# Attention memory with two MoE layers on one core: token order of the last block's gates, its stores on two queues, its last products by tile

## The chip, the cores and the metric

The kernel runs on one core of a Trainium2 chip. The metric is the device time of one execution in microseconds; the median of three runs stands for a kernel. A profile of one more execution gives the span from the first to the last instruction of the core, with every instruction and DMA in it.

## What is computed

Three parts follow on each other. An attention with a memory of 32 slots (4 batches, 8 heads, 576 positions, 64 features a head) gives x of 2304 tokens by 512 features. A gated layer (`_moe_ref`) normalizes x and takes it through 1536 gates back to 512. The last layer, which the change touches, is this:

```python
def _moe2_ref(x, w_in, w_out):          # x: (2304, 512), w_in: (512, 2048), w_out: (2048, 512)
    h = x @ w_in
    beta = 1.0
    neg = h <= -beta
    pos = h >= beta
    g = np.where(pos, h, np.where(neg, 0.0, (h + beta) ** 2 / (4.0 * beta)))
    return (g @ w_out).astype(np.float32)
```

Inputs and output are float32. The kernel splits each operand of a product into a high part, rounded to the matmul's type, and the rest (gh and gl, wh and wl, xh and xl), and takes three products for one: high by high, high by low, low by high.

## The kernel before

The first part and the gated layer are laid out by a planner with costs and due times (`Agenda`). The change touches neither. Their result x lies in DRAM as two matrices, high and low, of 512 features by 2304 tokens. The tokens stand there in an order of their own: first, for each batch, its 512 first positions (in the order j, p, where the position is 4p + j), then the last 64 positions of all four batches (in the order batch, j, p, where the position is 512 + 2p + j, with j of 2 and p of 32).

The last layer runs over five blocks of tokens: blocks 0 to 3 are the 512 first positions of a batch each, block 4 holds the 4 times 64 rest tokens, 256 in all. In a block it runs over 16 chunks of 128 gates (fc).

`p2_in(i, fc)` makes the gates of chunk fc for block i: twelve matmuls (L1032) into a PSUM tile hp, of 512 or 256 columns; then ScalarE's relu into y (L1037), two VectorE steps on y (L1038, L1039), ScalarE's rounding of y into gh (L1042) and VectorE's y minus gh into gl (L1043). In all of them the tokens stand in x's order, so a step is one run of columns.

`p2_out(i, fc)` multiplies a chunk's gates by w_out: for each tile t of 128 tokens (four, in block 4 two) three matmuls (L1057), gh by wh, gh by wl and gl by wh, of 512 columns each, are summed in the PSUM tile acc of t. A tile's sum is complete with chunk 15. It is then copied into osb, for even t by ScalarE (L1066), for odd t by VectorE (L1064), and stored from SyncE's queue. In blocks 0 to 3 that is one store of 128 rows of 2 KB (L1069), every fourth row of the output. In block 4 a tile holds two batches, 64 partitions each, with all 32 tokens of j = 0 ahead of those of j = 1; so there are two stores (L1073), and each writes the rows as j, p, features, which on the DRAM side is 2 by 32 by 512.

The loop at L1084 calls `p2_in` of a chunk and then `p2_out` of the chunk two before it (LAG). The last two rounds have no `p2_in` left: `p2_out` of chunks 14 and 15 of block 4. This part isn't laid out by hand. The framework puts each engine's instructions in an order of its own, by the order of the program and by what its timing model takes to be ready. It also adds the waits.

Of the kernel before, what the change touches and what calls it, by code (L numbers as in the profile page):

```python
# [8 lines left out]
F32R = mybir.dt.float32r  # L9
# [5 lines left out]
P = 128  # L15
# [134 lines left out]
def tile_attn_moe(tc, q, k, v, phi, w_gate, w_val, w_out1, rms_g, w_in2, w_out2, out):  # L150
# [10 lines left out]
    nc = tc.nc  # L161
    B, H, S, D = q.shape
# [11 lines left out]
    SM = P * QJ  # L174
    SL = S - SM
    LJ = 2
# [14 lines left out]
    def pool(stack, name, side):  # L191
        return stack.enter_context(tc.tile_pool(name=name, bufs=1, side=side))
# [772 lines left out]
    def load_w2(i, wp, **place):  # L965
        t = wp.tile([P, 2, 512], F32R, name=f"w2_{i}", **place)
        nc.gpsimd.dma_start(out=t.rearrange("p t f -> p (t f)"), in_=w2_d[i])
        wts[i % 2, i // 2] = (t[:, 0, :], t[:, 1, :])
# [27 lines left out]
    p2g = pool(right, "p2g", "right")  # L996
# [4 lines left out]
    def load_x(i):  # L1001
        c, n = blocks[i]
        xs = []
        for nm, src in (("h", x2h_d), ("l", x2l_d)):
            t = (xb if i else xa).tile([P, KC, SM], F32R, tag=f"x{nm}", name=f"x{nm}{i}", bufs=2 if i else 1)
            nc.gpsimd.dma_start(
                out=t[:, :, 0:n], in_=src[:, c : c + n].rearrange("(c p) t -> p c t", p=P)
            )
            xs.append(t)
        x_t[i] = xs  # L1010
# [11 lines left out]
    xb = pool(left, "xb", "left")  # L1022
    g_t = {}

    def p2_in(i, fc):
        c, n = blocks[i]
        xh, xl = x_t[i]
        wh, wl = (t.rearrange("p (c f) -> p c f", c=KC) for t in wts[0, fc])
        hp = psum.tile([P, 512], F32, tag=f"b{4 + (fc * 2 + fc // 2 % 2) % 4}", name=f"hp{i}_{fc}")[:, 0:n]
        for kc in range(KC):  # L1030
            for x, (wt, xt) in enumerate(((wh, xh), (wh, xl), (wl, xh))):
                nc.tensor.matmul(  # L1032
                    out=hp, lhsT=wt[:, kc, :], rhs=xt[:, kc, 0:n],
                    start=(kc == 0 and x == 0), stop=(kc == KC - 1 and x == 2),
                )
        y = p2.tile([P, SM], F32, tag="y2", name=f"y2_{i}_{fc}", bufs=2)[:, 0:n]
        nc.scalar.activation(out=y, in_=hp, func=AF.Relu, scale=0.5, bias=half)  # L1037
        nc.vector.scalar_tensor_tensor(out=y, in0=y, scalar=1.0, in1=y, op0=ALU.min, op1=ALU.mult)  # L1038
        nc.vector.tensor_tensor(out=y, in0=y, in1=hp, op=ALU.max)  # L1039
        gh = p2g.tile([P, SM], F32R, tag="gh", name=f"gh{i}_{fc}", bufs=2)[:, 0:n]  # L1040
        gl = p2g.tile([P, SM], F32R, tag="gl", name=f"gl{i}_{fc}", bufs=2)[:, 0:n]
        nc.scalar.activation(out=gh, in_=y, func=AF.Copy)  # L1042
        nc.vector.tensor_tensor(out=gl, in0=y, in1=gh.bitcast(F32), op=ALU.subtract)  # L1043
        g_t[i, fc] = (gh, gl)

    acc_t = {}

    def p2_out(i, fc):
        c, n = blocks[i]
        gh, gl = g_t.pop((i, fc))  # L1050
        wh, wl = wts[1, fc]
        if fc == 0:
            acc_t[i] = [psum.tile([P, 512], F32, tag=f"b{t}", name=f"acc{i}_{t}") for t in range(n // P)]
        for t, acc in enumerate(acc_t[i]):
            cs = slice(P * t, P * t + P)
            for x, (gt, wt) in enumerate(((gh, wh), (gh, wl), (gl, wh))):
                nc.tensor.matmul(  # L1057
                    out=acc, lhsT=gt[:, cs], rhs=wt,
                    start=(fc == 0 and x == 0), stop=(fc == NF2 - 1 and x == 2),
                )  # L1060
            if fc == NF2 - 1:
                o = p2.tile([P, DM], F32, tag="osb", name=f"osb{i}_{t}", bufs=2)
                if t % 2:
                    nc.vector.tensor_copy(out=o, in_=acc)  # L1064
                else:
                    nc.scalar.activation(out=o, in_=acc, func=AF.Copy)  # L1066
                if i < B:
                    dst = out[S * i : S * i + SM, :].rearrange("(p j) d -> j p d", j=QJ)[t]
                    nc.sync.dma_start(out=dst, in_=o)  # L1069
                else:  # L1070
                    for z in range(2):
                        r0 = S * (2 * t + z) + SM
                        nc.sync.dma_start(  # L1073
                            out=out[r0 : r0 + SL, :].rearrange("(p j) d -> j p d", j=LJ),
                            in_=o[SL * z : SL * z + SL, :],
                        )

    for i in range(EARLY, NF2):
        load_w2(2 * i, w2b)
    load_x(1)  # L1080
    load_x(2)
    LAG = 2
    seq = [(i, fc) for i in range(len(blocks)) for fc in range(NF2)]
    for z in range(len(seq) + LAG):  # L1084
        if z < len(seq):
            p2_in(*seq[z])
        if z >= LAG:
            p2_out(*seq[z - LAG])
            i, fc = seq[z - LAG]
            if fc == NF2 - 1 and 0 < i and i + 2 < len(blocks):  # L1090
                load_x(i + 2)
        if z == EARLY:
            for fc in range(N2U + N2R, NF2):
                load_w2(2 * fc + 1, wv, tag="raw", bufs=BUFS["raw"])
        if z == NF2 - 1:
            for fc in range(EARLY):
                load_w2(2 * fc, w2b)
# [36 lines left out]
```

## Time and profile before

| what | us |
|---|---|
| median of three runs | 884.05 |
| lowest and highest run | 882.97 and 884.27 |
| the profiled execution | 881.78 |
| its span | 880.0 |
| TensorE busy in the span | 828.8 (94%) |
| VectorE, ScalarE, GpSimd busy | 473.4, 350.8, 179.8 |

The engines have short names in the rows: PE is TensorE's matmul, PEld its weight load, DVE is VectorE, ACT ScalarE, POOL GpSimd, SP SyncE; a q behind a name is the engine's instruction queue, where it issues DMAs and waits. L1057 is line 1057 of the kernel before. A matmul's end is modelled and overlaps the start of the next one. Times of a row are microseconds from the span's start unless a column says ns. A DMA share is the mean busy share of the core's sixteen DMA engines.

### The profile page before, as it was taken

The page shows a single profiled execution, that of the slowest core. Times are in us where ns is not written, and L with a number is a line of the kernel's source. Part 1 is how long each engine was busy: PE and PEld are TensorE (multiplying, and loading weights), DVE is VectorE, ACT ScalarE, POOL GpSimd, SP SyncE. Part 2 cuts the span into 40 slices and gives each one's busy share as a digit, 9 for nine tenths or more (in the row PEclk, how much of TensorE's full clock was granted, in tenths as well). Part 3 has the DMA queues.
Part 4 walks back from the last instruction along what each step waited for, and adds up shares of the span by engine and source line. Part 5 has one row for each costly group of instructions (what it writes and reads, how often), then busy time and mean ns, then how long its engine had stood idle before and what let it go on. Part 6 is the DMA issues. An engine that isn't in the chain of part 4 may idle for free.

```text
span 880.0 us, 15147 instructions
## 1 busy us (share of the span) xinstructions
PE 828.8 (94%) x6058; PEld 724.1 (82%) x6058; DVE 473.4 (54%) x817; ACT 350.8 (40%) x695; POOL 179.8 (20%) x207
## 2 busy tenths in 40 slices
PE   7996797799999999999999999999999999999993
PEld 5885576589999999999998888888888888888892
DVE  3679989974875488357413333433343334333441
ACT  1466786752664477356302222222222222222331
POOL 3257855431312222123303200000000000000000
PEclk9999899699999999999999999999999999999997
DMA  9965757747578688776956920100040003000100
GB/s 323 327 203 187 244 192 262 271 140 245 192 252 305 223 277 275 238 250 228 353 195 209 400 93 1 48 1 0 5 140 1 0 5 91 1 0 1 48 1 24
DMA packets 72143, 137.56 MB, mean 156 GB/s; under 512 B 8841, under 2 KB 37513, under 8 KB 72073
## 3 DMA queue, kind: packets, MB, share of 16 engines
q1 hardware_dynamic: 61576, 108.28, 36.4%
q0 software_dynamic: 10496, 28.32, 10.3%
q8 instruction: 47, 0.77, 0.4%
q14 instruction: 24, 0.19, 0.1%
HBM read 99.35 MB, written 37.22 MB: 155 GB/s over the span
## 4 chain that ended last, share of the span: by engine, by line
PE 85%; DVE 6%; DMA 2%; issue 2%; ACT 2%; POOL 1%; SPq 0%; POOLq 0%; DVEq 0%; ACTq 0%
PE acc L1057 23%; PE hp L1032 23%; PE ops L864 17%; PE vps L806 7%; PE gps L806 7%; PE vwps L757 2%; PE xp L678 1%; DMA kv<-in_v_dram 1%; PE sc L615 1%; DVE w L258 1%; DMA raw<-in_moe_w_val_dram 1%; PE kvps L489 1%; PE qps L597 1%; DVE w L267 1%; POOL cx L279 1%
## 5 line engine op out<-in xcount | busy, mean ns | idle before, releaser
L1032 PE MATMUL hp<-xh,w 128*128 128x512 f32 (+1 forms) x640 | 193.2, 369 | 0.0
L1057 PE MATMUL acc<-w,gh 128*128 128x512 f32 x576 | 178.5, 391 | 0.0
L1032 PEld LDWEIGHTS hp<-xh,w 128*128 128x128 f32 x640 | 117.0, 188 | 21.4
L1038 DVE SCALAR_TENSOR_TENSOR y<-y 128x512 f32<-128x512 f32 (+1 forms) x80 | 51.1, 639 | 151.8 <-ACT y L1037 151.8
L1057 PEld LDWEIGHTS acc<-w,gh 128*128 128x128 f32 x576 | 107.0, 188 | 22.4
L1032 PE MATMUL hp<-xl,w 128*128 128x512 f32 (+1 forms) x320 | 118.3, 370 | 0.0
L864 PE MATMUL ops<-ah,wo1h 128*128 128x288 f32 x384 | 113.6, 296 | 0.0
L864 PE MATMUL ops<-ah,wo1l 128*128 128x288 f32 x384 | 113.2, 295 | 0.0
L864 PE MATMUL ops<-al,wo1h 128*128 128x288 f32 x384 | 113.1, 295 | 0.0
L1057 PE MATMUL acc<-w,gl 128*128 128x512 f32 x288 | 112.7, 392 | 0.0
L1037 ACT ACTIVATE y<-hp,consts 128x512 f32<-128x512 f32 (+1 forms) x80 | 51.6, 645 | 151.5 <-PE hp L1032 151.5
L1042 ACT ACTIVATE gh<-y 128x512 fp32r<-128x512 f32 (+1 forms) x80 | 47.1, 589 | 137.7 <-PE acc L1057 120.3
L1043 DVE TENSOR_TENSOR gl<-y,gh 128x512 fp32r<-128x512 f32 (+1 forms) x80 | 51.1, 639 | 80.2 <-ACT gh L1042 80.2
L279 POOL TENSOR_TENSOR cx<-cx,raw 128x512 f32<-128x512 f32 x43 | 58.8, 1368 | 131.0 <-ACT raw L277 90.7
L864 PEld LDWEIGHTS ops<-ah,wo1h 128*128 128x128 f32 x384 | 72.0, 188 | 1.7 <-issue 1.7
L864 PEld LDWEIGHTS ops<-al,wo1h 128*128 128x128 f32 x384 | 72.1, 188 | 0.0
L864 PEld LDWEIGHTS ops<-ah,wo1l 128*128 128x128 f32 x384 | 72.0, 188 | 0.0
L1032 PEld LDWEIGHTS hp<-xl,w 128*128 128x128 f32 x320 | 60.3, 188 | 10.7
L806 PE MATMUL vps<-Ah,vwh 128*128 128x288 f32 x192 | 60.4, 315 | 7.2 <-DVE th L834 7.2
L1057 PEld LDWEIGHTS acc<-w,gl 128*128 128x128 f32 x288 | 54.0, 188 | 12.3
L806 PE MATMUL gps<-Ah,vwh 128*128 128x288 f32 x192 | 58.7, 306 | 4.0 <-ACT vwh L775 2.1
L806 PE MATMUL gps<-Ah,vwl 128*128 128x288 f32 x192 | 58.2, 303 | 3.7 <-DVE vwl L777 3.7
(115 smaller groups left out, 1411.1 us busy)
## 6 DMA issues: line engine op xcount, KB each, us to landing
w<-wf_d SPq DMA_DIRECT2D x36, 512.0 KB, 5.5
w<-w_d POOLq DMA_DIRECT2D x36, 512.0 KB, 9.4
w_d<-w2s SPq DMA_DIRECT2D x32, 512.0 KB, 3.4
raw<-in_moe_w_out_dram SPq DMA_DIRECT2D x28, 512.0 KB, 5.6
raw<-in_moe_w_in_dram SPq DMA_DIRECT2D x16, 512.0 KB, 5.1
raw<-in_moe_w_gate_dram SPq DMA_DIRECT2D x12, 512.0 KB, 5.3
raw<-in_moe_w_val_dram SPq DMA_DIRECT2D x12, 512.0 KB, 5.1
wf_d<-w SPq DMA_DIRECT2D x12, 512.0 KB, 3.1
```

Of the source, the lines that this page charges most:

```text
L258: nc.vector.tensor_scalar(out=dst, in0=hv, scalar1=SHRINK, scalar2=None, op0=ALU.mult)
L267: nc.vector.scalar_tensor_tensor(out=du, in0=du, scalar=3, in1=low, op0=ALU.logical_shift_left, op1=ALU.bitwise_or)
L279: nc.gpsimd.tensor_tensor(out=dst, in0=dst, in1=hv, op=ALU.mult)
L757: nc.tensor.matmul(out=vps[g][0][32 * c : 32 * c + 32, 2 * P * x : 2 * P * x + 2 * P], lhsT=vT[b][hs, c, :], rhs=t[hs, c].rearrange("p i f ...
L806: nc.tensor.matmul(out=p[:, 0:HB], lhsT=wt[:, g, i, :], rhs=at[b][:, g, c], start=(g == 0 and x == 0), stop=(g == 1 and x == 2),)
L864: nc.tensor.matmul(out=p[:, 0:HB], lhsT=wt[:, fc, d], rhs=at[:, c], start=(fc == 0 and x == 0), stop=(fc == NF1 - 1 and x == 2),)
L1032: nc.tensor.matmul(out=hp, lhsT=wt[:, kc, :], rhs=xt[:, kc, 0:n], start=(kc == 0 and x == 0), stop=(kc == KC - 1 and x == 2),)
L1037: nc.scalar.activation(out=y, in_=hp, func=AF.Relu, scale=0.5, bias=half)
L1038: nc.vector.scalar_tensor_tensor(out=y, in0=y, scalar=1.0, in1=y, op0=ALU.min, op1=ALU.mult)
L1042: nc.scalar.activation(out=gh, in_=y, func=AF.Copy)
L1043: nc.vector.tensor_tensor(out=gl, in0=y, in1=gh.bitcast(F32), op=ALU.subtract)
L1057: nc.tensor.matmul(out=acc, lhsT=gt[:, cs], rhs=wt, start=(fc == 0 and x == 0), stop=(fc == NF2 - 1 and x == 2),)
```

## The change

In block 4, y is viewed as batch, j, p and gh and gl as batch, p, j, so that L1042 and L1043 write the gates in the order of the output's rows. The matmuls of L1057 then leave 64 output rows of a batch in 64 partitions in order, and each store of block 4 writes 64 whole rows that lie in one piece; the second one of each tile is issued on ScalarE's queue. The last two rounds of the loop become one: chunks 14 and 15 for tile 0, then both for tile 1. LAG is only moved, and `g_t` keeps its entries, since a pair of gates is now fetched once for each tile.

```diff
@@ -1037,21 +1039,27 @@
-        gh = p2g.tile([P, SM], F32R, tag="gh", name=f"gh{i}_{fc}", bufs=2)[:, 0:n]
-        gl = p2g.tile([P, SM], F32R, tag="gl", name=f"gl{i}_{fc}", bufs=2)[:, 0:n]
+        gh = p2g.tile([P, SM], F32R, tag="gh", name=f"gh{i}_{fc}", bufs=LAG)[:, 0:n]
+        gl = p2g.tile([P, SM], F32R, tag="gl", name=f"gl{i}_{fc}", bufs=LAG)[:, 0:n]
+        g_t[i, fc] = (gh, gl)
+        if i == B:
+
+            y = y.rearrange("q (b j p) -> q b j p", b=B, j=LJ)
+            gh, gl = (t.rearrange("q (b p j) -> q b j p", b=B, j=LJ) for t in (gh, gl))
         nc.scalar.activation(out=gh, in_=y, func=AF.Copy)
         nc.vector.tensor_tensor(out=gl, in0=y, in1=gh.bitcast(F32), op=ALU.subtract)
-        g_t[i, fc] = (gh, gl)
...
-    def p2_out(i, fc):
+    def p2_out(i, fc, only=None):
         c, n = blocks[i]
-        gh, gl = g_t.pop((i, fc))
+        gh, gl = g_t[i, fc]
...
         for t, acc in enumerate(acc_t[i]):
+            if only not in (None, t):
+                continue
...
                     for z in range(2):
                         r0 = S * (2 * t + z) + SM
-                        nc.sync.dma_start(
-                            out=out[r0 : r0 + SL, :].rearrange("(p j) d -> j p d", j=LJ),
-                            in_=o[SL * z : SL * z + SL, :],
+                        (nc.scalar if z else nc.sync).dma_start(
+                            out=out[r0 : r0 + SL, :], in_=o[SL * z : SL * z + SL, :]
                         )
...
     for z in range(len(seq) + LAG):
         if z < len(seq):
             p2_in(*seq[z])
-        if z >= LAG:
+        if z >= len(seq):
+
+            if z == len(seq):
+                for t in range(len(acc_t[B])):
+                    for x in range(z - LAG, z):
+                        p2_out(*seq[x], t)
+        elif z >= LAG:
             p2_out(*seq[z - LAG])
```

## Rows read from the trace of the kernel before

**Rows 1.** Busy time by stretch: its ends, length, each engine's time, clock, DMA share, GB/s.
```profile
818.60:865.30 46.70, 46.61 (x289) 41.58 (x287) 20.78 (x49) 15.10 (x34) 0.00 (x0) 1.00 0.06 23
865.30:880.00 14.70, 0.00 (x0) 0.00 (x0) 0.64 (x1) 0.32 (x1) 0.00 (x0) 0.58 0.10 36
```

**Rows 2.** The chain that ended last, from 855 on: start, length, what.
```profile
858.26 1.40 PE acc L1057 x6
859.65 1.43 PE hp L1032 x12
861.09 4.14 PE acc L1057 x18
...
865.25 0.69 DVE osb L1064
```

**Rows 3.** Busy time by stretch, behind the last matmul (columns as in rows 1).
```profile
872.00:873.00 1.00, 0.00 (x0) 0.00 (x0) 0.00 (x0) 0.00 (x0) 0.00 (x0) 0.50 0.13 51
...
878.40:878.50 0.10, 0.00 (x0) 0.00 (x0) 0.00 (x0) 0.00 (x0) 0.00 (x0) 0.50 0.06 21
```

**Rows 4.** DMA traffic: packets of 865 to 880, then of 821 to 824.
```profile
DMA packets 264, 0.52 MB, mean 35 GB/s; under 512 B 8, under 2 KB 8, under 8 KB 264
...
DMA packets 288, 0.52 MB, mean 175 GB/s; under 512 B 32, under 2 KB 32, under 8 KB 288
```

**Rows 5.** The close of the program, from 868: durations ns, first and last start.
```profile
L1129 SPq DRAIN  x3: 7/7/7, 879.2 to 879.5; - x3
```

**Rows 6.** Busy time by stretch as a store of L1069 begins (columns as in rows 1).
```profile
822.30:822.40 0.10, 0.10 (x2) 0.10 (x1) 0.00 (x0) 0.00 (x0) 0.00 (x0) 1.00 0.38 143
822.40:822.50 0.10, 0.10 (x2) 0.09 (x1) 0.00 (x0) 0.00 (x0) 0.00 (x0) 1.00 1.02 389
```

**Rows 7.** Order of time, ACT and DVE, last chunk: start, length, what, idle before.
```profile
861.18 0.47 ACT L1037 ACTIVATE y<-hp,consts 128x256 f32<-128x256 f32 x1 [0.93 <-PE hp L1032]
...
862.15 0.42 DVE L1039 TENSOR_TENSOR y<-y,hp 128x256 f32<-128x256 f32 x1
862.66 0.42 ACT L1042 ACTIVATE gh<-y 128x256 fp32r<-128x256 f32 x1 [1.01 <-DVE y L1039]
863.12 0.43 DVE L1043 TENSOR_TENSOR gl<-y,gh 128x256 fp32r<-128x256 f32 x1 [0.54 <-ACT gh L1042]
865.02 0.60 ACT L1066 ACTIVATE osb<-acc 128x512 f32<-128x512 f32 x1 [1.94 <-PE acc L1057]
```

**Rows 8.** Order of time, SyncE's queue: an issue of L1069, then two of L1073's four.
```profile
821.51 0.33 SPq L1069 DMA_DIRECT2D out_dram<-osb  x1
...
865.64 0.67 SPq L1073 DMA_DIRECT2D out_dram<-osb  x1
...
867.58 0.74 SPq L1073 DMA_DIRECT2D out_dram<-osb  x1
```

**Rows 9.** From the stores of osb by line: time to landing, of L1069's sixteen.
```profile
DMA to landing us min/median/max: 2.1/2.4/4.6
```

**Rows 10.** DMA issues by GpSimd, one of two groups: ns min/median/max, starts.
```profile
L1006 POOL DMA_DIRECT2D xl<-x2l_d x5: 740/747/800, 433.5 to 723.9; - x5
```

**Rows 11.** Order of time, PE, chunk 14's products (chunk 15's alike); and the weight loads' mean (ns).
```profile
862.32 1.08 PE L1057 MATMUL acc<-w,gh 128*128 128x512 f32 x4
863.23 0.62 PE L1057 MATMUL acc<-w,gl 128*128 128x512 f32 x2
...
L1057 PEld LDWEIGHTS acc<-w,gh 128*128 128x128 f32 x576 | 107.0, 188 | 22.4
```

**Rows 12.** Instructions by form: count, busy us, mean ns, idle before.
```profile
L261 ACT ACTIVATE raw<-raw 128x512 uint32<-128x512 uint32 x45 | 30.3, 678 | 5.5 <-DMA raw<-in_moe_w_in_dram 3.7 <-DMA raw<-in_moe_w_out_dram 1.7
L1042 ACT ACTIVATE gh<-y 128x512 fp32r<-128x512 f32 x64 | 40.4, 632 | 120.0 <-PE acc L1057 117.0 <-DVE y L1039 3.0
L412 DVE TENSOR_REDUCE pm<-phi 128x128 f32<-128x1152 f32 x4 | 8.6, 2142 | 4.1 <-DMA phi<-in_phi_dram 4.1
L441 DVE TENSOR_TENSOR phi<-phi,mps 128x1152 f32<-128x1152 f32 x4 | 5.4, 1349 | 1.1 <-PE mps L435 1.1
```

More of the change, by code (lines that the diff above doesn't have):

```diff
@@ L1023, in tile_attn_moe @@
     g_t = {}
+    LAG = 2
     def p2_in(i, fc):
@@ L1081, in tile_attn_moe @@
     load_x(2)
-    LAG = 2
     seq = [(i, fc) for i in range(len(blocks)) for fc in range(NF2)]
```

## Prediction

> **What bounds the kernel now.** I read the page first, then the busy time of three stretches at the end, then the chain of waits, then the DMA traffic in steps of a microsecond. In the last block TensorE has no gap: 46.61 of 46.70 us busy between 818.6 and 865.3 [rows 1]. Behind it come 14.7 us, a sixtieth of the span, in which only stores move. The chain ends with the matmuls of L1057 at 865.22 and the VectorE copy of the second output tile, 865.25 to 865.94 [rows 2]; the rest up to 880.0 is the four stores of L1073 and the close of the program.
>
> These stores are slow. In the slice from 872, one of six alike, they move 51 GB/s at a DMA share of 0.13 [rows 3], and 0.13 of 16 engines is two. The packet count says the same: 264 packets are 256 rows of 2 KB and 8 packets under 512 B, so two small ones for each of four stores; the two stores of L1069 in the window from 821 have 256 rows and 32 small ones, sixteen each [rows 4]. I read the small packets as one for each engine that takes part. The form that differs is the outermost dimension: 2 (the j of L1074) against 128 rows. So 0.52 MB at 51 GB/s take 10.3 us, and this is what the change can act on. It can't act on the closing: the last byte moves in the slice up to 878.5, at about 878.45, the SyncE queue's first drain is at 879.2 [rows 3, 5], and from there to 880.0 it is 0.8. That is 1.55 from the last byte to the end.
>
> **The change, part by part.** The profiled execution took 881.78, its span 880.0. The sum is made in the span; what lies around it (1.78) I leave as it is. The median of the runs is 884.05, that is 2.27 above the profiled one, so I take the difference of the spans from 884.05.
>
> *Whole rows.* Each store now has 64 rows as its outermost dimension, on both sides. No row of the trace has 64. The two ends are the two-engine stores (51 GB/s) and L1069's (389 GB/s in a full slice [rows 6]); I take the latter, since what the two differ in is the size of the outer dimension, and 64 is, like 128, far above 16 and divides evenly over it.
> The Trainium skill says how many engines take part ("DMA: Bandwidth & Descriptors", section "Why a DMA increments its semaphore by 16 and not by 1"): the largest number up to 16 that divides the slowest dimension of both sides. By that, 2 for the old form, 16 for L1069, as the small packets show, and 16 for 64 rows, which no run here shows; the sum would be the same.
>
> Now the times. The ScalarE copy of tile 0 ends at 865.62 and its first store is issued at 865.64 [rows 7, 8]. An issue of L1069 holds the queue 0.33, two of L1073's four 0.67 and 0.74 [rows 8]; I take 0.33, as the new form has plain rows like L1069. The first bytes of L1069's store, issued 821.51, are in the slice from 822.3 [rows 6, 8]: some 0.5 after the end of the issue. So tile 0's bytes flow from 866.47, and 256 KB at 389 GB/s take 0.68: to 867.15. Tile 1 is copied at 865.94, its stores are issued at 866.0 to 866.33 and could flow from 866.8; they queue behind tile 0's bytes and flow from 867.15 to 867.83. With the 1.55 behind the last byte as before: 869.4. L1069's median landing gives about the same: 866.0 + 2.4 [rows 9], 0.35 for the queueing and 0.8 of closing are 869.55.
>
> *Two queues.* The store of each tile's second batch (z = 1, partitions 64 to 127) goes from SyncE's queue to ScalarE's. On SyncE alone four issues of 0.33 would end at 865.64 + 1.32 = 866.96; 0.5 later, at 867.46, the last 128 KB could flow, which is when the three stores ahead of them are through (866.47 + 1.01). So at 0.33 an issue the second queue is worth nothing; at L1073's 0.67 it is worth 1.3 (four issues to 868.32, last byte 869.16 instead of 867.83). I take nothing, since I took 0.33. ScalarE's sequencer issues no DMA in this trace, so its price is bounded: from below by 0.33, from above by GpSimd's 0.74 to 0.80 [rows 10], the only other engine that issues any. I take 0.33 (same form of store), with 0.75 in the range. The second of these issues waits for VectorE's copy of tile 1; nothing is queued behind it on ScalarE, whose last work is the copy of tile 0 [rows 7].
>
> *Products tile by tile.* Now the last two chunks (fc 14 and 15) go over tile 0 first, then tile 1: the same 12 matmuls. The order that TensorE ran before is not the written one: in both chunks four products with gh and then two with gl [rows 11], where the text has gh, gh, gl for each tile. So the order is chosen from estimated readiness, and the rewritten loop may come out as before or as written. As before it costs and brings nothing. As written, tile 0's products with chunk 15 start three matmuls of 0.23 after 862.32, at 863.01, but its gh ends on ScalarE at 863.08 [rows 7]; with a hop of 0.09 (VectorE's end 862.57 to ScalarE's start 862.66 [rows 7]) and a weight load of 0.19 ahead [rows 11], the matmul starts at 863.36: a stall of 0.35. Its gl is ready at 863.55 and, after the stall, its weight load is wanted at 863.6, so no second stall. TensorE would then end at 865.6 instead of 865.2, but tile 0's stores would be gone before tile 1's come, which gives back the 0.35 of queueing. So the end is 869.4 to 869.75; the cover for this zero is the traffic of tile 0.
>
> *Gates in the tokens' order.* In the 16 chunks of block 4, L1042 writes gh with a step of two elements, L1043 reads it so and writes gl so. No instruction is added. ScalarE's L261 reads and writes with that step: 678 ns for 512 elements, against 632 of L1042 [rows 12], 1.07 times. VectorE has no strided write; its nearest row is L412, which reads with a long step: 2142 ns for 1152 elements against 1349 of L441, 1.6 times [rows 12]. So gh 0.42 becomes 0.45 to 0.67, gl 0.43 becomes 0.43 to 0.68. A chunk takes 2.83 on TensorE (1.43 and 1.40 [rows 2]); of that ScalarE works 0.89 and VectorE 1.28 (three steps of some 0.43) [rows 7]. A chunk's gates are ready 2.5 after its hp ends (861.09 to 863.55 [rows 2, 7]), and its own products come two chunks later, 5.6 after: hidden by 3 us. Only the last chunk has no further hp ahead of it; there, in the order as before, gh is wanted at 863.5 and ready at 863.08, still hidden, and in the written order its extra 0.03 to 0.25 adds to the stall. I take nothing and keep 0.1 for the range. A gain is excluded, since contiguous is the best of these rows.
>
> *Sum*: 880.0 to 869.4, that is 10.6 less; 884.05 - 10.6 = 873.45, rounded to 873.5. Bounds of this case: all of tile 0's traffic out of the way and the fastest landing of L1069 (2.1 from issue [rows 9]): 866.0 + 2.1 + 0.8 = 868.9, 872.95; with a stall of 0.35, gates 0.1 later and issues of 0.67: tile 1's copy ends at 866.4, its issues at 867.1, its bytes flow from 867.6 to 868.3, and the end is 869.85, 873.9. The runs before spread by 1.3, half of which goes on either side: 872.3 to 874.6.
>
> **The rivals.**
> *Half the engines* (0.07). If a store from 64 partitions got half of L1069's rate, and the two halves of a tile didn't make up for each other: 0.52 MB at 194 GB/s take 2.7 from 866.47, 869.17, with 1.55 behind it 870.7: 874.75. For it: no row shows a store from 64 partitions at full rate. Against it: the two halves go at once, on two queues.
> The Trainium skill speaks for it ("SBUF — State Buffer", section "Door 1: The DMA port swizzle"): partitions 0 to 63 reach 8 of 16 ports, 64 to 127 the other 8, so a store from 64 gets half the rate; side by side they would get all of it. No store here from 64 partitions shows that yet.
>
> *ScalarE's queue is late* (0.11). If its issues take 0.75, the second starts at 866.39, and if that first use of a queue lands as slowly as the slowest of L1069 (4.6 [rows 9]), it lands at 871.0, and the end is 871.8: 875.85. For it: the queue has carried nothing in this kernel. Against: SyncE's own row has a median of 2.4.
>
> *The stores aren't spread* (0.04). If the 64 rows, being one contiguous piece of memory, still ran on two engines, 10.3 us from 866.47 give 876.8 to 878, and 878.35 to 879.55 with the close: 882.4 to 883.6, within 0.2%. Against: L1069's form.
>
> *The gates become the bound* (0.02), slower. If the strided gh took so long that ScalarE sets the chunk, block 4 grows sixteenfold by the excess. It begins at 2.83 - 0.47 = 2.36 for gh, and decides from 10.6 + 1.8 = 12.4 lost, 0.78 a chunk, gh at 3.1 us, 7.5 times its 0.42: 885.85 and up. The strided rows show 1.07 to 1.6 times [rows 12].
>
> **How the numbers follow.** My case has 0.76. Its time is 873.5. The range goes from 872.2 to 875.4: it holds nearly all of this case, the half-engines case and the lower half of the late-queue case; out are the unspread stores, the slow gates, the upper half of the late queue and some of my own case, about 0.19. About 0.2% (1.77 us) is what a measurement of this kernel can tell from no change. Faster is my case, the half engines and the late queue: 0.94; within 0.2% the unspread stores: 0.04; slower the gates: 0.02.
>
> **What would show it.** In the profile after: the stretch from TensorE's end to the span's end at 4 to 5 us instead of 14.8; a DMA share near 0.9 in it, not 0.13; 16 small packets for each store, 64 for the four; two DMA issues on ScalarE's queue, of 0.33 to 0.75; gh near 0.45 and gl near 0.43; block 4's chunk at 2.83 still; and at the last chunk either TensorE's old order or a gap of about 0.4. Wrong it would be if the share stayed low, if ScalarE's two stores landed microseconds behind SyncE's, or if the chunks of block 4 grew.

## The result and the profile after

| | before | after |
|---|---|---|
| median of 4 runs, us | 883.51 | 873.15 |
| lowest and highest, us | 881.72 and 884.27 | 871.83 and 875.82 |
| ratio, 95% interval | | 0.9893 (0.9872 to 0.9914) |
| profiled execution, its span, us | 881.78, 880.0 | 873.91, 872.1 |
| end of the last matmul to end of the span, us | 14.8 | 5.2 |

By the medians the kernel is 10.4 us faster, by the ratio of the runs 9.5 (0.9893 of 883.5); the forecast was 873.5. I call the last line of the table the tail: it is the measure of this case, because the span ahead of the tail differs from run to run by more than the changes tried here. L806's first gps product, for one, begins at 105.9 in the trace before and at 107.8 in the one after, with the same code ahead of it, and between 105.5 and 107.8 over thirteen traces of this study. So the two spans differ by 7.9 only, while the tails differ by 9.6.

The chain of waits after, its last pieces (start, length, what), which answer to [rows 2]:

```profile
862.77 4.14 PE acc L1065 x18
866.90 0.02 issue
866.93 0.69 DVE osb L1072
```

The last 18 products take 4.14 as before. Then the order of time of the stores' issues, which answers to [rows 8]:

```profile
867.33 1.17 SPq L1081 DMA_DIRECT2D out_dram<-osb  x2
867.33 1.44 ACTq L1081 DMA_DIRECT2D out_dram<-osb  x2
```

The issues now run on both queues at once. The DMA traffic of the tail, by packets and by queue (packets, MB, share of sixteen engines in a window of 14.1 us), answers to [rows 4]:

```profile
DMA packets 320, 0.52 MB, mean 37 GB/s; under 512 B 64, under 2 KB 64, under 8 KB 320
...
q1 hardware_dynamic: 160, 0.26, 7.1%
q10 hardware_dynamic: 160, 0.26, 5.2%
```

64 small packets instead of 8: sixteen engines for each of the four stores instead of two. And the busy time by stretch (columns as in rows 1), which answers to [rows 3]:

```profile
868.00:868.50 0.50, 0.00 (x0) 0.00 (x0) 0.00 (x0) 0.00 (x0) 0.00 (x0) 1.00 0.00 0
868.50:869.20 0.70, 0.00 (x0) 0.00 (x0) 0.00 (x0) 0.00 (x0) 0.00 (x0) 1.00 0.90 187
869.20:869.85 0.65, 0.00 (x0) 0.00 (x0) 0.00 (x0) 0.00 (x0) 0.00 (x0) 1.00 1.07 394
868.50:870.55 2.05, 0.00 (x0) 0.00 (x0) 0.00 (x0) 0.00 (x0) 0.00 (x0) 1.00 0.84 255
```

The 0.52 MB take 2.05 us, 255 GB/s on average instead of 51. But there are two speeds in it: 187 GB/s at first, 394 in the middle, both at a share of 0.9 or more, and about 190 again at the end. The experiments take that up. From the last byte (870.55) to the end of the span it is 1.55, as before; the first drain of SyncE's queue, which answers to [rows 5], is at 871.3:

```profile
L1141 SPq DRAIN  x3: 7/7/7, 871.3 to 871.6; - x3
```

The order of time of TensorE's last two chunks, which answers to [rows 11], is the old one, four products with gh and two with gl; the tile-by-tile loop left no trace in it:

```profile
864.00 1.08 PE L1065 MATMUL acc<-w,gh 128*128 128x512 f32 x4
...
864.92 0.61 PE L1065 MATMUL acc<-w,gl 128*128 128x512 f32 x2
865.37 1.07 PE L1065 MATMUL acc<-w,gh 128*128 128x512 f32 x4
866.28 0.61 PE L1065 MATMUL acc<-w,gl 128*128 128x512 f32 x2
```

And the gates of block 4 in their new order, by form (count, busy us, mean ns, idle before), on ScalarE and VectorE; contiguous they took 0.42 and 0.43 [rows 7]:

```profile
L1049 ACT ACTIVATE gh<-y 128x256 fp32r<-128x256 f32 x14 | 6.1, 437 | 14.5 <-DVE y L1041 14.5
...
L1050 DVE TENSOR_TENSOR gl<-y,gh 128x256 fp32r<-128x256 f32 x15 | 6.4, 426 | 8.8 <-ACT gh L1049 8.8
```

### The profile page after: what moved, and what is told of

It reads as the page before. It is cut to its first block, busy times and chain, and to the rows that moved or that the text cites. A ratio compares the mean times of both kernels' runs of the same rounds, so it can differ in the third digit from the quotient of the medians.

```text
span 872.1 us, 15148 instructions
## 1 busy us (share of the span) xinstructions
PE 831.8 (95%) x6058; PEld 725.9 (83%) x6058; DVE 472.3 (54%) x817; ACT 351.1 (40%) x695; POOL 180.3 (21%) x207
## 3 DMA queue, kind: packets, MB, share of 16 engines
q0 software_dynamic: 10496, 28.32, 10.4%
## 4 chain that ended last, share of the span: by engine, by line
PE 86%; DVE 6%; ACT 3%; DMA 2%; issue 2%; POOL 1%; SPq 0%; DVEq 0%; ACTq 0%; POOLq 0%
PE acc L1065 23%; PE hp L1034 23%; PE ops L864 17%; PE vps L806 7%; PE gps L806 7%; PE vwps L757 2%; PE xp L678 2%; PE sc L615 1%; DMA kv<-in_v_dram 1%; DMA raw<-in_moe_w_val_dram 1%; PE kvps L489 1%; PE qps L597 1%; DVE w L258 1%; DVE w L267 1%; DVE cx L258 1%
## 5 line engine op out<-in xcount | busy, mean ns | idle before, releaser
L806 PE MATMUL vps<-Ah,vwh 128*128 128x288 f32 x192 | 60.1, 313 | 6.7 <-DVE th L834 6.5
L806 PE MATMUL gps<-Ah,vwh 128*128 128x288 f32 x192 | 59.0, 307 | 5.0 <-ACT vwh L775 3.0
L806 PE MATMUL gps<-Ah,vwl 128*128 128x288 f32 x192 | 58.3, 303 | 3.5 <-DVE vwl L777 3.5
```

The lines of the kernel that those rows point to most:

```text
L806: nc.tensor.matmul(out=p[:, 0:HB], lhsT=wt[:, g, i, :], rhs=at[b][:, g, c], start=(g == 0 and x == 0), stop=(g == 1 and x == 2),)
```

## The experiments

All of them in one table. "From chunk 14" is the time from the first product of chunk 14 to the end of the span, which also holds a gap on TensorE. Ratios are to the kernel before on the same chip, with their 95% intervals.

| kernel | tail, us | from chunk 14, us | ratio |
|---|---|---|---|
| before | 14.8 | 17.7 | 1 |
| after | 5.2 | 8.1 | 0.9893 (0.9872 to 0.9914) |
| e1, whole rows alone | 5.8 | 8.7 | 0.9894 (0.9878 to 0.9910) |
| e2, two queues alone | 15.5 | 18.4 | 1.0012 (1.0001 to 1.0022) |
| e4, whole rows and two queues, old loop | 5.2 | 8.1 | 0.9894 (0.9875 to 0.9913) |
| e5, old gates, stores of 32 rows | 6.3 | 9.2 | 0.9901 (0.9883 to 0.9919) |
| e6, after in the written order | 4.6 | 7.8 | 0.9872 (0.9855 to 0.9890) |
| e7, one store for each tile | 4.8 | 7.7 | 0.9891 (0.9870 to 0.9913) |
| e8, e7 by hand, copy on two engines | 4.7 | 7.7 | 0.9887 (0.9866 to 0.9908) |
| e9, before with 4 by 16 rows | 10.6 | 13.5 | single execution |
| e10, after by hand, copies swapped | 5.3 | 8.2 | 0.9886 (0.9870 to 0.9902) |
| e11, e1 from partitions 32 to 95 | 5.6 | 8.5 | single execution |
| e12, one store, by hand, copies swapped | 4.5 | 7.4 | 0.9890 (0.9874 to 0.9905) |

Each tail is that of one profiled execution. After and e4, which are the same program, agree in both columns to 0.1 us, and I take that as what a tail can tell. The ratios of the kernels with faster stores can't be told apart: their intervals overlap.

**e1: whole rows alone.** The changed kernel with the old loop and this store:

```diff
-                        (nc.scalar if z else nc.sync).dma_start(
+                        nc.sync.dma_start(
```

> Whole rows alone: the gates in the tokens' order and stores of 64 whole rows, all four on SyncE's queue, the loop as before. Measured by the tail, from the end of the last matmul to the end of the span: 14.8 us before (865.22 to 880.0), 5.2 after (866.90 to 872.1). Theory (the number of engines follows the outermost dimension, 64 rows go to sixteen): 64 small packets for the four stores, tail 5.2 to 6.6, the upper end if four issues of 0.54 in a row set it; the time within 1.5 us of the changed kernel. Rival (the second queue carries a good part of the gain): tail 9 or more. On the side: if a store from 64 partitions reaches only half of the paths, a store that flows alone moves about 200 GB/s at a share near 1; if not, about 390.

Of the 9.6 us, 9.0 are there: tail 5.8, from 865.52 to 871.3. The stores' issues by line (ns min/median/max, starts), and then the busy time of the stretch in which they flow one after another:

```profile
L1081 SPq DMA_DIRECT2D out_dram<-osb x4: 547/563/587, 865.9 to 867.8; - x4
```

```profile
867.10:869.70 2.60, 0.00 (x0) 0.00 (x0) 0.00 (x0) 0.00 (x0) 0.00 (x0) 0.58 0.91 201
867.10:867.50 0.40, 0.00 (x0) 0.00 (x0) 0.00 (x0) 0.00 (x0) 0.00 (x0) 1.00 0.99 220
```

An issue of 64 rows takes 0.55 on SyncE alone, with no other queue beside it, where L1069's 128 rows took 0.33 [rows 8]. And a store alone moves 201 to 220 GB/s at a share of 0.91 to 0.99: the sixteen engines are busy, but at half of L1069's pace [rows 6]. So the side question has its answer: about 200, not 390.

**e2: two queues alone.** The kernel before with this store:

```diff
-                        nc.sync.dma_start(
+                        (nc.scalar if z else nc.sync).dma_start(
                             out=out[r0 : r0 + SL, :].rearrange("(p j) d -> j p d", j=LJ),
```

> Two queues alone: the gates and the stores of 2 by 32 rows as before, the second store of each tile on ScalarE's queue. Theory (both queues use the same two engines): 8 small packets, DMA share 0.13, some 51 GB/s, tail 13.8 to 14.8, time as before within 1 us. Rival (the queues' stores run on different engines, or each queue has its own rate): share 0.25, some 100 GB/s, tail 9 to 10, time 5 us below before.

Neither: the tail got longer by 0.7, 867.44 to 882.9. The busy time of a stretch in the middle of it, and the issues on ScalarE by line:

```profile
875.00:876.00 1.00, 0.00 (x0) 0.00 (x0) 0.00 (x0) 0.00 (x0) 0.00 (x0) 0.50 0.13 51
```

```profile
L1077 ACTq DMA_DIRECT2D out_dram<-osb x2: 534/952/1371, 867.9 to 869.3; - x2
```

Same share, same 51 GB/s, and 8 small packets as before: both queues feed the same two engines. One of ScalarE's issues took 1.37. So a second queue alone brings nothing, as the theory had it, though it had not seen a price.

**e9: four engines.** The kernel before with another view of the same 64 rows:

```diff
-                            out=out[r0 : r0 + SL, :].rearrange("(p j) d -> j p d", j=LJ),
+                            out=out[r0 : r0 + SL, :].rearrange("(p j) d -> j p d", j=4),
```

> The kernel before with each of its four last stores written as 4 by 16 by 512 instead of 2 by 32 by 512, everything else as it was; the rows within a batch's last 64 land in another order. Theory (the number of engines is the outermost dimension): 16 small packets for the four stores, DMA share 0.25, some 102 GB/s, 5.1 us for the bytes, tail 9.3 to 10. Rival (rows with a step in DRAM are what costs): 51 GB/s still, tail 14 to 15.

The packets of the tail, and the busy time of one of its stretches:

```profile
DMA packets 272, 0.52 MB, mean 37 GB/s; under 512 B 16, under 2 KB 16, under 8 KB 272
```

```profile
872.00:873.00 1.00, 0.00 (x0) 0.00 (x0) 0.00 (x0) 0.00 (x0) 0.00 (x0) 0.50 0.26 102
```

Outer dimension 4: 16 small packets, a share of 0.26, 102 GB/s. In this stretch the rate is twice that of outer dimension 2, though the rows now step by four in DRAM. It isn't so all along: up to 871, long after the last issue (868.2), the stores moved 51 to 68 GB/s only, at the same share. Why they do is not shown. With it the tail is 10.6, 0.6 above what I had written. The rule of the Trainium skill cited in the prediction ("DMA: Bandwidth & Descriptors", section "Why a DMA increments its semaphore by 16 and not by 1") gives 2, 4 and 16 engines for these forms, and the traces agree with all three by the small packets: 8, 16 and 64 for four stores.

**e5: old gates, 32 rows a store.** The kernel before with

```diff
-                    for z in range(2):
-                        r0 = S * (2 * t + z) + SM
+                    for z in range(2 * LJ):
+                        r0 = S * (2 * t + z // LJ) + SM
                         nc.sync.dma_start(
-                            out=out[r0 : r0 + SL, :].rearrange("(p j) d -> j p d", j=LJ),
-                            in_=o[SL * z : SL * z + SL, :],
+                            out=out[r0 : r0 + SL, :].rearrange("(p j) d -> j p d", j=LJ)[z % LJ],
+                            in_=o[LP * z : LP * z + LP, :],
                         )
```

> The gates as before (columns in the order batch, j, p), but each store cut in two, one for each j: 32 rows of 2 KB, every second row of the output, eight stores on SyncE's queue. Theory (only the outermost dimension counts, 32 rows go to sixteen engines): 128 small packets; eight issues of 0.4 to 0.55 set the tail: 6 to 7.5 us, so most of the gain comes without the new order of the gates. Rival (the rows must lie in one piece in DRAM): the rate stays near 51 GB/s and the tail is 11 or more.

The packets of the tail, and the issues by line:

```profile
DMA packets 384, 0.52 MB, mean 37 GB/s; under 512 B 128, under 2 KB 128, under 8 KB 384
```

```profile
L1073 SPq DMA_DIRECT2D out_dram<-osb x8: 345/420/435, 869.1 to 872.3; - x8
```

Tail 6.3, with 128 small packets and eight issues of 0.345 to 0.435. So 8.5 of the 9.6 us come without any new order of the gates: what counts is that no store has an outer dimension of 2. The new order saves four issues, which is worth 0.5 (e1 against this).

**e11: which partitions.** e1 with the stores' source moved:

```diff
-                            out=out[r0 : r0 + SL, :], in_=o[SL * z : SL * z + SL, :]
+                            out=out[r0 : r0 + SL, :], in_=o[32:96, :]
```

> The kernel with whole rows alone (all four stores on SyncE's queue), but both stores of a tile read partitions 32 to 95 of the copied tile; partitions 0 to 31 and 96 to 127 aren't stored, and the rows of the last blocks are not the right ones. Rows, bytes, packets and queue are the same. With partitions 0 to 63 and 64 to 127 the four stores moved 201 GB/s at a share of 0.91. Theory (the Trainium skill, 'SBUF - State Buffer', section 'Door 1: The DMA port swizzle': a half of the partitions on one side of 64 reaches 8 of 16 ports, 32 to 95 reaches all): 350 to 400 GB/s within a store, a store's bytes in about 0.35 us, the last byte 0.2 to 0.4 earlier, since the issues of 0.55 then set the pace: tail 5.3 to 5.6. Rival (64 rows of 2 KB are too few to fill the engines, wherever they lie): 200 GB/s still and a tail of 5.8.

Two slices of stores that flow alone:

```profile
868.80:868.90 0.10, 0.00 (x0) 0.00 (x0) 0.00 (x0) 0.00 (x0) 0.00 (x0) 1.00 1.02 389
869.30:869.40 0.10, 0.00 (x0) 0.00 (x0) 0.00 (x0) 0.00 (x0) 0.00 (x0) 1.00 1.08 410
```

389 to 410 GB/s, with the same number of rows, packets and bytes and the same queue: for stores that follow each other on one queue the half rate hangs on the partitions. (Both stores of a tile read the same 64 here, so that nothing else had to change.) This is what the Trainium skill's rule gives ("SBUF — State Buffer", section "Door 1: The DMA port swizzle"): partitions 0 to 63 or 64 to 127 reach 8 ports of 16, and 32 to 95 lie across. The trace agrees, 201 against 389. The tail fell by only 0.2, to 5.6, since the four issues of 0.53 to 0.61 now set the pace.

**e4: the loop.** The changed kernel with `if z >= LAG: p2_out(*seq[z - LAG])` as before.

> The changed kernel with the loop of before: new gates' order, whole rows, two queues, but the last two rounds as they were. The framework's order of each engine's instructions is the same for both forms of the loop. Theory (the rewritten loop does nothing): tail 5.2 as in the changed kernel, four products with gh and two with gl for each of the last chunks, time within 0.2% of the changed kernel. Rival (the loop has a share in the gain): tail 5.6 or more.

As the theory has it: 5.2 and 8.1, the figures of the changed kernel. Over the last 39 us the two traces have the same instructions in the same order on TensorE, VectorE and ScalarE. So e4 is the changed kernel a second time, and its ratio, 0.9894, repeats the result in other runs.

**e6: the written order, held.** The changed kernel with its last twelve products under the framework's manual order:

```diff
             if z == len(seq):
+                hand = ExitStack()
+                hand.enter_context(tc.manual_schedule())
                 for t in range(len(acc_t[B])):
                     for x in range(z - LAG, z):
                         p2_out(*seq[x], t)
+                hand.close()
```

> The changed kernel with TensorE's last twelve products held to the written order: chunks 14 and 15 for tile 0, then for tile 1. In the changed kernel's trace the order was the one of before (four products with gh, two with gl, for each chunk), and from the first product of chunk 14 to the end of the span it took 8.1 us (864.00 to 872.1). Theory (the prediction's step): a stall of 0.3 to 0.45 before tile 0's first product with chunk 15, tile 0's stores about 0.5 us earlier against the last matmul, tail 4.5 to 5.0, and the 8.1 becomes 7.9 to 8.4. Rival (tile 0's stores out of the way are worth more than the stall): 7.6 or less.

TensorE's order of time, matmuls and the weight load with the wait:

```profile
864.66 0.40 PE L1065 MATMUL acc<-w,gl 128*128 128x512 f32 x1
865.03 0.73 PE L1065 MATMUL acc<-w,gh 128*128 128x512 f32 x2
865.60 0.39 PE L1065 MATMUL acc<-w,gl 128*128 128x512 f32 x1
...
865.03 0.30 PEld L1065 LDWEIGHTS acc<-w,gh 128*128 128x128 f32 x2 [0.41 <-ACT gh L1049]
```

The weight load waited for gh, and the twelve products took 3.16 (864.20 to 867.36) instead of 2.90: a stall of 0.26, against 0.35 by the prediction's step and at least 0.3 by the expectation. Tile 0's stores were through by 869.0, before tile 1's began at 869.2. Together it is 0.3 less than the changed kernel, 7.8, between the theory's range and the rival's: the stores out of the way are worth more than the stall, but not by as much as the rival had. So in this one profile the tile order is worth something once it is really run, which in the changed kernel it isn't.

**e7, e8: one store for each tile.** In e7, gh and gl of block 4 are written in the order p, j, batch, so that a tile holds 32 rows of all four batches:

```diff
-            gh, gl = (t.rearrange("q (b p j) -> q b j p", b=B, j=LJ) for t in (gh, gl))
+            gh, gl = (t.rearrange("q (p j b) -> q b j p", b=B, j=LJ) for t in (gh, gl))
...
-                    for z in range(2):
-                        r0 = S * (2 * t + z) + SM
-                        (nc.scalar if z else nc.sync).dma_start(
-                            out=out[r0 : r0 + SL, :], in_=o[SL * z : SL * z + SL, :]
-                        )
+                    dst = out.rearrange("(b s) d -> s b d", b=B)[SM + 32 * t : SM + 32 * t + 32]
+                    (nc.scalar if t else nc.sync).dma_start(out=dst, in_=o)
```

> One store for each tile instead of two: gh and gl of block 4 are written in the order p, j, batch (a step of eight elements along p), so a tile holds 32 rows of all four batches, and its store is 32 by 4 by 512 from 128 partitions; tile 0's goes out on SyncE's queue, tile 1's on ScalarE's. Theory (a store from 64 partitions runs at half rate, as the stores that flowed alone showed at 200 GB/s; one from 128 doesn't): 32 small packets, near 390 GB/s from the first byte, last byte about 1.4 us after the first, tail 4.2 to 4.6. Rival (what costs is the issue and the fixed latency alone): the rate no better than in the changed kernel, tail 5.0 to 5.3.

The busy time of the stretch with all 0.52 MB, an issue by line, and the gates with a step of eight by form:

```profile
869.30:870.75 1.45, 0.00 (x0) 0.00 (x0) 0.00 (x0) 0.00 (x0) 0.00 (x0) 0.60 0.97 362
```

```profile
L1080 SPq DMA_DIRECT2D out_dram<-osb x1: 662/662/662, 868.0 to 868.0; - x1
```

```profile
L1049 ACT ACTIVATE gh<-y 128x256 fp32r<-128x256 f32 x15 | 10.6, 709 | 15.7 <-DVE y L1041 14.5 <-PE acc L1065 1.2
```

The rate is as the theory had it, 362 on average over both stores. The tail is 4.8, above my 4.2 to 4.6: this form's issue takes 0.66. The wide step costs, too: gh went from 0.42 to 0.71, hidden here by TensorE.

e8 adds a hand order (chunk 14 tile 0, chunk 14 tile 1, chunk 15 tile 0, chunk 15 tile 1) and shares tile 1's copy:

```diff
+                if i == B and t:
+                    nc.vector.tensor_copy(out=o[:, 0:256], in_=acc[:, 0:256])
+                    nc.scalar.activation(out=o[:, 256:512], in_=acc[:, 256:512], func=AF.Copy)
```

> As the one-store kernel, with the last twelve products held in the order chunk 14 tile 0, chunk 14 tile 1, chunk 15 tile 0, chunk 15 tile 1, and the copy of tile 1 shared by VectorE (columns 0 to 255) and ScalarE (256 to 511). Theory: no gap on TensorE, tile 0 complete 0.7 instead of 0.23 before the last matmul, tile 1's copy 0.42 instead of 0.69, tail 3.5 to 4.0, the fastest of all by 1 us or more over the changed kernel. Rival (the two halves of the copy take turns, as they read one bank): copy 0.8 in all, tail 3.9 to 4.4.

The copies, in order of time:

```profile
867.96 0.42 DVE L1072 COPY osb<-acc 128x256 f32<-128x256 f32 x1 [1.28 <-PE acc L1065]
868.42 0.39 ACT L1073 ACTIVATE osb<-acc 128x256 f32<-128x256 f32 x1 [0.55 <-DVE osb L1072]
```

The rival's case for the copy: ScalarE's half began when VectorE's had ended, and its row names VectorE's write of osb as what released it; 0.85 in all against 0.69 for one copy. Whether the chip needs that wait or the framework only orders it wasn't tried. The tail of 4.7 lies above both ranges, and the gain of 1 us over the changed kernel didn't come: the ratios are 0.9887 and 0.9893.

**e10: by hand, copies swapped.** The changed kernel with e8's order, and tile 0 copied by VectorE, tile 1 by ScalarE:

```diff
-                if t % 2:
+                if t % 2 != (i == B):
```

> The changed kernel with the last twelve products held in the order chunk 14 tile 0, chunk 14 tile 1, chunk 15 tile 0, chunk 15 tile 1, and the copies swapped: tile 0 on VectorE (0.69), tile 1 on ScalarE (0.60). Theory: no gap on TensorE, tile 0's stores out of the way, so 4.4 to 4.7 from the end of the last matmul and 7.3 to 7.6 from the first product of chunk 14 to the end (8.1 in the changed kernel, 7.8 with the written order). Rival (no cover is left over from the order): 7.9 or more.

The rival's number came, 8.2, with a cause that I hadn't named. ScalarE's order of time:

```profile
867.84 0.57 ACTq L1081 DMA_DIRECT2D out_dram<-osb  x1
868.62 0.60 ACT L1074 ACTIVATE osb<-acc 128x512 f32<-128x512 f32 x1 [2.96 <-DVE osb L1072]
```

TensorE was done at 867.77, but tile 0's second store stood ahead of tile 1's copy on ScalarE. It waited for VectorE's copy of tile 0, took 0.57 to issue, and the copy began 0.85 late. In the changed kernel ScalarE has no copy left by then, so its issues hold up none.

**e12: one store, by hand, copies swapped.** e10 with one store for each tile, so that ScalarE issues only behind its own copy. The gates of each tile are written by two instructions, with a step of four:

```diff
+            for t in range(2):
+                ys = y[:, P * t : P * t + P].rearrange("q (b j p) -> q b j p", b=2, j=LJ)
+                hs, ls = (g[:, P * t : P * t + P].rearrange("q (p j b) -> q b j p", b=2, j=LJ) for g in (gh, gl))
+                nc.scalar.activation(out=hs, in_=ys, func=AF.Copy)
+                nc.vector.tensor_tensor(out=ls, in0=ys, in1=hs.bitcast(F32), op=ALU.subtract)
...
+                    dst = out[2 * S * t : 2 * S * t + 2 * S, :].rearrange("(b s) d -> s b d", b=2)
+                    (nc.scalar if t else nc.sync).dma_start(out=dst[SM:S], in_=o)
```

> As the last one, and one store for each tile from 128 partitions: the gates of each tile are written in the order p, j, batch (a step of four elements along p), in two instructions for each of gh and gl, and the store is 64 by 2 by 512. Theory (rate 390 GB/s, issue 0.66 as in the other one-store kernel): tail 4.1 to 4.4, 7.0 to 7.3 from the first product of chunk 14, the shortest end of all; in the runs' time 1 us below the changed kernel, which is about what they can tell. Rival (the second instruction for each gate delays chunk 15's products): a gap on TensorE before chunk 15, 7.6 or more.

The shortest end of all, 4.5 and 7.4, though 0.1 above both of my ranges. There is no gap on TensorE (2.91 for the twelve products, 862.69 to 865.60). In the runs' time its ratio, 0.9890, can't be told from the changed kernel's, so I don't call it the faster kernel.

## Why the prediction was right, and where it was off

The time was right, 873.15 against 873.5, and so was the step that carries it: the old tail's bytes are the work of two engines, and 64 rows go to sixteen. e9, e5 and e1 show it by doubling the outer dimension, by cutting the stores and by the rows alone. The close, 1.55, and the chunk, hidden gates included, stayed. gh went from 0.42 to 0.44, just below the 0.45 to 0.67 that I had.

The 10.3 us of bytes in the prediction are too short. From the first byte (866.9) to the last (878.45) the old stores took 11.5, since they began well below 51 GB/s:

```profile
866.80:867.20 0.40, 0.00 (x0) 0.00 (x0) 0.00 (x0) 0.00 (x0) 0.00 (x0) 1.00 0.10 20
...
867.60:868.00 0.40, 0.00 (x0) 0.00 (x0) 0.00 (x0) 0.00 (x0) 0.00 (x0) 0.63 0.14 15
```

The sum isn't touched by this, as it takes the end of the span before and not that term.

The sum's terms for the stores were mis-sized, together by 1.0: the forecast's tail is 4.2 (869.4 less 865.22), the measured one 5.2. The rival "half the engines", to which I gave 0.07, had a tail of 5.5 (870.7 less 865.22), nearer to it.

- *The issue*, taken as 0.33, took 0.53 to 0.55 on SyncE and 0.57 to 0.78 on ScalarE. I had put the form "plain rows" beside L1069's. e1 shows 0.55 with nothing beside it. With a first byte 0.62 behind the issue instead of 0.5, this is 0.35.
- *The bytes*, taken at 389 GB/s from both tiles, 1.36, took 2.05 at 255: the other 0.7. The step that failed is the choice of L1069's rate for a source of 64 partitions. That rival had much of the mechanism, though not the engines' number: all sixteen work, at half rate each (e1), unless the source lies across partition 64 (e11) or fills all partitions (e7). On two queues the two halves make up for part of it: a tile's pair takes 1.0 us, against 1.3 one after the other (e1) and 0.68 in the sum.
- *The second queue*, taken as worth nothing, was worth 0.6 (5.8 to 5.2, e1 to after). How much of that is the overlap of the issues and how much the rate isn't separated, but e11 points to the issues: with every store at the full rate one queue's tail is still 5.6. The Trainium skill ("DMA: Bandwidth & Descriptors", section "Issuing engines are not separate DMA queues") has it that a second issuing engine saves issue time only. The rate over all four stores, 255 against 201, fits that only as far as e1's pace is set by its issues. They come about every 0.6, and a store's bytes take 0.65 there, so no run here shows that the issue time is all. ScalarE's issues cost what the late-queue rival had, up to 0.78, but no store landed later than 3.0 after its issue, against that rival's 4.6.

*Products tile by tile*: of the two outcomes in the prediction the one without effect came (e4). The stall that I had worked out for the other is 0.26 (e6), not 0.35.

Why did the median come out within 0.4 of the forecast all the same, with 1.0 too much gain in the sum? That was luck. The sum has a gain of 10.6 and the medians differ by 10.4, but the tails by 9.6 only, and the ratio of the runs gives 9.5. e4, the same program in other runs, is 9.0 below the kernel before by its medians (873.31 against 882.27). The rest lies ahead of the tail, where the runs before spread by 2.6 us and those after by 4.0; the range had been given half of 1.3 for this, too little.

## What to carry to other kernels

Count a store's small packets, or look at the DMA share behind the last matmul: here a share of 0.13 came from an outermost dimension of 2, and a view or a cut that gave it a multiple of sixteen took 8.5 to 9.0 us off the tail, where a second queue alone took none. Stores from half of the partitions, one after the other on a queue, ran at half rate (201 against 389 GB/s), and one transfer from all 128 didn't (362). Look for computing work behind an issue on a computing engine's queue: in e10 a copy stood there and began 0.85 late.

## What the runs showed of the hardware that I had not expected

- The issue's price depends on the form, and not by the rows alone: 0.33 for 128 rows of 2 KB [rows 8], 0.35 to 0.44 for 32 rows (e5), 0.48 to 0.61 for 64 rows on SyncE (e1, e6, e11), 0.66 for 32 by 4 and for 64 by 2 rows (e7, e12). Why 64 rows cost more than 128 stays open.
- With two queues not every store from 64 partitions runs at half rate. In the kernel after, the first of a burst moves at 187 GB/s (868.5 to 869.2). The second, ScalarE's, then goes at the full rate; these are the packets by queue of 869.2 to 869.5 (packets, MB, share of sixteen engines):

```profile
DMA packets 75, 0.12 MB, mean 410 GB/s; under 512 B 15, under 2 KB 15, under 8 KB 75
...
q10 hardware_dynamic: 59, 0.12, 103.8%
q1 hardware_dynamic: 16, 0.00, 7.2%
```

By the records of the two queues the second store begins only when the first is nearly through. What it does in the meantime they don't show, and why it is then not held to half rate stays open.

- ScalarE and VectorE write a step of two 4-byte elements at nearly full pace (437 against 417 ns, 426 against 425) and a step of eight at 1.7 and 1.6 times (709 and 681 ns). The Trainium skill ("SBUF — State Buffer", section "Door 1: The DMA port swizzle", in its note on SBUF's lines of 16 bytes) has steps of up to four fp32 free and wider ones not. The traces agree at two and at eight. At four e12 speaks against it: its gates of 128 elements take 441 ns on ScalarE, where L711, a copy of the same size that writes runs of 64 elements, takes 270. These are the two by form, from e12's trace:

```profile
L1049 ACT ACTIVATE gh<-y 128x128 fp32r<-128x128 f32 x32 | 10.8, 441 | 17.7 <-DVE y L1041 14.5 <-PE acc L1068 3.2
...
L711 ACT ACTIVATE Ah<-ATp 128x128 fp32r<-128x128 f32 x4 | 1.1, 270 | 1.2 <-PE ATp L702 1.2
```

L711 reads PSUM and the gates' copy reads SBUF, so the two differ in more than the step, and the step's share isn't separated.
